# An adaLN attention and gMLP block on one core: gate statistics deferred, another order of the start, part of the transposes by DMA, the last bias by TensorE, the closing branch turned

## The chip, the cores and the metric

One Trainium2 chip, one of its cores. The metric is the device time of one execution in microseconds (us), the median of several runs. A ratio is the mean time of one kernel's fast runs over the mean of the kernel before's fast runs of the same rounds on the same chip, so it isn't quite the ratio of the medians quoted; the brackets behind it are its 95% interval. Times inside a profile are counted from the span's start; the span, first to last instruction, is some 2 us shorter than the device time.

## The reference

```python
mod = (silu(c) @ w_mod)                  # sa, ca, ga, sb, cb, gb: six rows of 512
h = layernorm(x) * (1 + ca) + sa         # x: 2048 x 512 bf16 ("LN1")
q = h @ wq                               # 32 heads of 128; K and V come from a cache, 8 groups
p = softmax(q k^T / sqrt(128)); o = p v  # every query sees all 2048 keys
x = x + ga * (o @ wo)
h = layernorm(x) * (1 + cb) + sb         # "LN2"
z = gelu(h @ w_in)                       # 2048 x 1792: z1 | z2
z2 = layernorm(z2)
g = w_sp @ z2 + b_sp                     # "spatial": mixes the 2048 rows
x = x + gb * ((z1 * g) @ w_out)
```

## The kernel before

A *unit* is 128 rows of queries of one group (four heads). There are 128 units. Each has eight *slots*, and work can be hung onto a slot with `at(unit, slot, fn)`:

```python
    for it in range(NU + 6):                     # NU = 128
        ...
        for i in range(NSLOT):                   # 8 slots
            for fn in later.pop((it, i), []): fn()
            if it < NU: qk(it, i)                # 2 score matmuls, 1 exponential (ScalarE)
            if 1 <= it <= NU: pv(it - 1, i)      # 8 value matmuls of the unit before
            for fn in fill.pop((it, i), []): fn()        # projection matmuls of later q
            if i >= 4 and wf: wf[i - 4]()                # output projection
            if it >= NU: zrun(3)                 # z2 and z1 matmuls fill up the last units
```

What the change touches. The order at the start:

```python
    def ln1_at(it, ch):                          # LN1 of 512 rows, "chunk" ch
        st = {}
        at(it, 1, lambda: st.update(r=ln1_stats(ch * CT, CT)))           # DVE
        at(it, 5, lambda: st.update(x=ln1_norm(ch * CT, CT, st["r"])))   # DVE
        at(it, 7, lambda: ln1_turn(ch * CT, CT, st["x"]))  # PE transposes, PSUM to hT on DVE
    at(0, 0, lambda: ln1_turn(1, CT - 1, xns0))  # rows 128 to 511
    for i in range(NSLOT):
        fill[0, i] = rest0[2 * i : 2 * i + 2]    # their projections
    ln1_at(0, 1); ln1_at(2, 2); ln1_at(5, 3)     # shortened
    at(3, 0, mod_rest)                           # rest of the modulation rows
```

The statistics of z2, straight behind each tile, and the normalisation behind each fourth:

```python
            nc.scalar.activation(out=z2[:, j, :]..., func=ACT.Gelu_apprx_tanh)
            stz = stat.tile([P, NFHC, nc.vector.BN_STATS_DIM], FP32, name="stz")
            for h in range(NFHC):
                nc.vector.bn_stats(out=stz[:, h, :], in_=z2[:, j, h * FC : (h + 1) * FC])
            nc.vector.bn_aggr(out=mvz[:, j, :], in_=stz[:])
    ...
        if j % CT == CT - 1:
            zq[-1] = [zq[-1], lambda ch=j // CT: z2_norm(ch)]
```

The spatial bias, added on VectorE for each tile, and the branch at the end, which runs a slower general path only if a safety flag was set (it isn't for these inputs):

```python
        nc.vector.tensor_tensor(out=gb[:, :n], in0=g_ps[:, :n], in1=bsp_bc[:, cols], op=ALU.add)
        nc.vector.tensor_tensor(out=yT[:, f, c0 : c0 + n], in0=gb[:, :n], in1=z1T[:, f, cols], op=ALU.mult)
    ...
    redo = nc.values_load(flag[0:1, 0:1], min_val=0, max_val=P)
    with tc.If(redo != 0):
        general_path(...)
```

Of the kernel before, what the change touches and what calls it, by code (L numbers as in the profile page):

```python
# [15 lines left out]
P = 128  # L16
# [559 lines left out]
def kernel(  # L576
# [45 lines left out]
    v_dram = A_v_cache[0].rearrange("g (t p) d -> p g t d", p=P)  # L622
    k_rows = A_k_cache[0].rearrange("g (p t) d -> p g t d", p=P)
    v_rows = A_v_cache[0].rearrange("g (p t) d -> p g t d", p=P)
    wmod_dram = w_mod.rearrange("(dt p) n -> p dt n", p=P)
# [72 lines left out]
    k_nat = early.tile([P, SK], BF16, name="kT")  # L698
    nc.sync.dma_start(out=k_nat[:].rearrange("p (t d) -> p t d", d=DH), in_=k_rows[:, 0])
    nc.sync.dma_start(out=x_sb[:, 1:CT, :], in_=x_dram[:, 1:CT, :])  # L700

# [7 lines left out]

    def load_v(g, rows, engine):  # L710
        v1 = late.tile([P, NKT, DV], BF16, name="v1")
        nc.gpsimd.memset(v1[:, :, DH:DV], 1.0)  # L712
        engine.dma_start(out=v1[:, :, 0:DH], in_=rows[:, g])
        groups[g]["v1"] = v1
# [13 lines left out]
    load_wq(0, nc.sync)  # L728
    groups[0] = {}
    load_v(0, v_rows, nc.sync)  # L730
    nc.sync.dma_start(out=x_sb[:, CT : 2 * CT, :], in_=x_dram[:, CT : 2 * CT, :])
    nc.sync.dma_start(out=wmod_b, in_=wmod_dram[:, :, 2 * D : NMOD])
    nc.sync.dma_start(out=x_sb[:, 2 * CT : NT, :], in_=x_dram[:, 2 * CT : NT, :])
    load_wo(0, nc.sync)
    nc.sync.dma_start(out=win_sb[:], in_=win_dram)


    c_f = res.tile([P, NDT], FP32, name="c_f")
    nc.vector.tensor_copy(out=c_f[:], in_=c_bf[:])
# [8 lines left out]
    nc.vector.tensor_copy(out=sc_bf[:], in_=sc[:])  # L748
    nc.vector.memset(ones_bf[:], 1.0)

    def mod_columns(first, wmod, i0):

        mc_ps = bank("o_ps")
        for i in range(2):
            for dt in range(NDT):
                col = i * NDT + dt
                w0 = (first + i - i0) * D + dt * P
                for kt in range(NDT):
                    nc.tensor.matmul(
                        mc_ps[:, col : col + 1],  # L760
                        lhsT=wmod[:, kt, w0 : w0 + P],
                        rhs=sc_bf[:, kt : kt + 1],
                        start=(kt == 0),
                        stop=(kt == NDT - 1),
                    )
        c0 = first * NDT
        nc.vector.tensor_copy(out=modc[:, c0 : c0 + NDT], in_=mc_ps[:, 0:NDT])
        nc.vector.tensor_scalar_add(
            out=modc[:, c0 + NDT : c0 + 2 * NDT], in0=mc_ps[:, NDT : 2 * NDT], scalar1=1.0
        )  # L770
# [14 lines left out]

    def ln1_turn(j0, n, xns):
        ch, c0 = j0 // CT, (j0 % CT) * P
        if ch not in hTs:
            hTs[ch] = res.tile([P, NDT, 512], BF16, name="hT", bufs=NCH)
        hT = hTs[ch]  # L790
        for half in range(2):
            t_ps = bank("misc")[:].bitcast(BF16).rearrange("p (k q) -> p k q", k=2)
            for k in range(2):
                dt = half * 2 + k
                for jj in range(n):
                    nc.tensor.transpose(  # L796
                        t_ps[:, k, jj * P : (jj + 1) * P],
                        xns[jj][:, dt * P : (dt + 1) * P],
                        ident[:],
                    )  # L800
            for k in range(2):
                dt = half * 2 + k
                nc.vector.tensor_scalar(  # L803
                    out=hT[:, dt, c0 : c0 + n * P],
                    in0=t_ps[:, k, 0 : n * P],
                    scalar1=modc[:, NDT + dt : NDT + dt + 1],
                    scalar2=modc[:, dt : dt + 1],
                    op0=ALU.mult,
                    op1=ALU.add,
                )  # L810

    xns0 = ln1_norm(0, 1, ln1_stats(0, 1))
    mod_columns(0, wmod_a, 0)
    ln1_turn(0, 1, xns0)


    kT0 = early.tile([P, SK], BF16, name="kT")
    groups[0]["kT"] = kT0
    k_ps = bank2()[:].bitcast(BF16)
    for kt in range(NKT):  # L820
        nc.tensor.transpose(
            k_ps[:, kt * P : (kt + 1) * P], k_nat[:, kt * P : (kt + 1) * P], ident[:]
        )
    for hf in range(2):
        nc.scalar.copy(
            out=kT0[:, hf * SK // 2 : (hf + 1) * SK // 2],
            in_=k_ps[:, hf * SK // 2 : (hf + 1) * SK // 2],
        )
    rstd0 = ln1_stats(1, CT - 1)

# [28 lines left out]
    for fn in qproj(0, list(range(REP)), 0, P):  # L859
        fn()  # L860
    xns0 = ln1_norm(1, CT - 1, rstd0)

# [126 lines left out]

    def mod_rest():  # L990
        mod_columns(3, wmod_b, 2)
        lhs = []
        for kt in range(NDT):
# [4 lines left out]
            lhs.append(lhs_bc)  # L998
        for row_out, i in ((ga_rows, 2), (gb_rows, 5)):
            mr_ps = bank("misc")  # L1000
            for kt in range(NDT):
                nc.tensor.matmul(
                    mr_ps[:],
                    lhsT=lhs[kt][:],
                    rhs=wmod_b[:, kt, (i - 2) * D : (i - 1) * D],
                    start=(kt == 0),
                    stop=(kt == NDT - 1),
                )
            nc.vector.tensor_copy(out=row_out[:], in_=mr_ps[:])

# [7 lines left out]

    def ln1_at(it, ch):
        st = {}  # L1020
        at(it, 1, lambda: st.update(r=ln1_stats(ch * CT, CT)))
        at(it, 5, lambda: st.update(x=ln1_norm(ch * CT, CT, st["r"])))
        at(it, 7, lambda: ln1_turn(ch * CT, CT, st["x"]))

    fill = {}
    rest0 = qproj(0, list(range(REP)), P, 512 - P)
    at(0, 0, lambda: ln1_turn(1, CT - 1, xns0))
    for i in range(NSLOT):
        fill[0, i] = rest0[2 * i : 2 * i + 2]
    ln1_at(0, 1)  # L1030
    ln1_at(2, 2)
    ln1_at(5, 3)
    at(3, 0, mod_rest)

    def set_fill(b):

        fs = qproj(b, list(range(REP)), 0, 512)
        for k, fn in enumerate(fs):
            it, slot = ((b - 1) * CT + k // NDT, k % NDT) if b > 1 else (1 + k // 8, k % 8)
            fill.setdefault((it, slot), []).append(fn)  # L1040
# [7 lines left out]
    for g in range(1, HKV):  # L1048
        it = (g - 1) * NT + 4
        at(it, 3, lambda g=g: load_k(g))  # L1050
        at(it + 1, 3, lambda g=g: load_v(g, v_dram, nc.gpsimd))
        at(it + 2, 3, lambda g=g: load_wo(g, nc.gpsimd))
# [5 lines left out]
    def z2_tile(j):  # L1058
        ps = {}

        def mm(hf, dt):
# [16 lines left out]
            )  # L1078
            stz = stat.tile([P, NFHC, nc.vector.BN_STATS_DIM], FP32, name="stz")
            for h in range(NFHC):  # L1080
                nc.vector.bn_stats(out=stz[:, h, :], in_=z2[:, j, h * FC : (h + 1) * FC])  # L1081
            nc.vector.bn_aggr(out=mvz[:, j, :], in_=stz[:])

        return [lambda hf=hf, dt=dt: mm(hf, dt) for hf in range(NFHC) for dt in range(NDT)]

    def z2_norm(ch):
# [30 lines left out]
    for j in range(3 * CT):  # L1117
        zq += z2_tile(j)
        if j % CT == CT - 1:
            zq[-1] = [zq[-1], lambda ch=j // CT: z2_norm(ch)]  # L1120
    for f in range(NFT):
        zq += z1_tile(f, 0)
    zq = [z if isinstance(z, list) else [z] for z in zq]

    def zrun(n):
        for _ in range(min(n, len(zq))):
            for fn in zq.pop(0):
                fn()

# [38 lines left out]
    for j in range(3 * CT, NT):  # L1168
        for fn in z2_tile(j):
            fn()  # L1170
    z2_norm(3)
    for f in range(NFT):
# [27 lines left out]

    def spatial(t, yT, f, c0, n):

        g_ps = bank("misc")
        for st in range(NT):
            nc.tensor.matmul(  # L1205
# [3 lines left out]
                start=(st == 0),  # L1209
                stop=(st == NT - 1),  # L1210
            )
        cols = slice(t * 512 + c0, t * 512 + c0 + n)
        gb = mlp.tile([P, 512], BF16, name="gb", bufs=2)
        nc.vector.tensor_tensor(out=gb[:, :n], in0=g_ps[:, :n], in1=bsp_bc[:, cols], op=ALU.add)  # L1214
        nc.vector.tensor_tensor(
            out=yT[:, f, c0 : c0 + n], in0=gb[:, :n], in1=z1T[:, f, cols], op=ALU.mult
        )
# [10 lines left out]
    def finish_tile(t, jj, src, parts=1):  # L1228
# [4 lines left out]
        for k in range(parts):  # L1233
            s = slice(k * w, (k + 1) * w)
            nc.vector.tensor_tensor(out=tmp[:, s], in0=src[:, s], in1=gb_rows[:, s], op=ALU.mult)
            nc.vector.tensor_tensor(out=yout[:, s], in0=tmp[:, s], in1=x_sb[:, j, s], op=ALU.add)
            (nc.sync if k == 0 else nc.scalar).dma_start(out=out_dram[:, j, s], in_=yout[:, s])

# [34 lines left out]
    for f in range(NFT):  # L1273
        spatial(last, yT, f, n_a, P)
        if f == 0:
# [10 lines left out]
    redo = nc.values_load(flag[0:1, 0:1], min_val=0, max_val=P)  # L1286
    with tc.If(redo != 0):
        general_path(
# [33 lines left out]
```

## Time and profile before

| kernel before | us |
|---|---|
| median time (3 runs, 1347.53 to 1349.29) | 1348.0 |
| span of the profiled run | 1345.2 |
| first score of unit 1 starts | 27.66 |
| first score of unit 4 starts | 58.76 |
| first z2 matmul starts | 1150.16 |
| first spatial matmul starts | 1213.63 |
| last VectorE operation ends | 1340.59 |

The rows mark where a part of the program ends. The difference of two kernels from one mark to the next tells where time was won or lost. Where the work of one line on one engine is shown (L1287 is the line of the final branch, SP the sync engine), the columns are line, engine, operation, count, then duration in ns (shortest/median/longest), first and last start in us.

```profile
L1287 SPq EVENT_SEMAPHORE  x8: 17/17/17, 1342.8 to 1343.3; - x8
...
L1287 SPq COMPARE_BRANCH  x1: 53/53/53, 1340.2 to 1340.2; - x1
```

SP branches once at 1340.2, and its next instruction, a semaphore wait, starts at 1342.8. In these 2.6 us the last output DMAs land, so they cost nothing of their own.

### The profile page before, as it was taken

How to read it: one execution, taken by the hardware profiler on the slowest of the kernel's cores; microseconds unless marked ns; L12 is line 12 of the kernel's file. 1: busy time of each engine (PE TensorE's matmuls, PEld its weight loads, DVE VectorE, ACT ScalarE, POOL GpSimd, SP SyncE). 2: the span in 40 equal slices, each digit the busy share in tenths (PEclk: the TensorE clock that was granted, in tenths of full speed). 3: DMA queues.
4: the chain of work that ended last, by engine and by line, in shares of the span. 5: the costliest groups of instructions: out<-in, count | busy, mean ns of one | idle time of the engine just before them, and what ended most of it. 6: DMA issues, size and time to landing. Idle time of an engine off the chain costs nothing.

```text
span 1345.2 us, 27642 instructions
## 1 busy us (share of the span) xinstructions
PE 1303.1 (97%) x12137; PEld 860.4 (64%) x12345; DVE 476.3 (35%) x1171; ACT 1079.2 (80%) x1059; POOL 46.4 (3%) x88
## 2 busy tenths in 40 slices
PE   6999999999999999999999999999999999979997
PEld 4666666666666666666666666666666666534444
DVE  5442222222222222222222222222222666873344
ACT  4789999999999999999999999999999999540000
POOL 1010000000000000000000000000000000110000
PEclk9999999999999999999999999999999999989999
DMA  8120021102211120012010410121111111143200
GB/s 274 29 64 17 13 63 37 21 17 35 62 20 21 32 68 17 17 37 68 17 20 13 84 21 17 21 64 32 21 20 17 29 29 33 25 110 83 67 20 26
DMA packets 141184, 56.53 MB, mean 42 GB/s; under 512 B 131105, under 2 KB 136353, under 8 KB 141057
## 3 DMA queue, kind: packets, MB, share of 16 engines
q1 hardware_dynamic: 137504, 42.17, 15.0%
q0 software_dynamic: 3408, 12.45, 3.5%
q8 instruction: 98, 1.61, 0.5%
q14 instruction: 30, 0.24, 0.1%
q10 hardware_dynamic: 144, 0.07, 0.0%
HBM read 21.63 MB, written 2.10 MB: 18 GB/s over the span
## 4 chain that ended last, share of the span: by engine, by line
PE 92%; DVE 3%; SPq 2%; issue 1%; DMA 1%; POOL 0%; ACT 0%; ACTq 0%; POOLq 0%; DVEq 0%
PE s_ps L879 35%; PE o_ps L901 34%; PE misc L843 7%; PE misc L933 6%; PE misc L1205 6%; PE s_ps L1100 2%; SPq L1012 1%; PE o_ps L1220 1%; PE s_ps L1064 1%; DMA wq_g<-in_A_wq_dram 1%; DVE stz L1081 1%; DVE hT L803 0%; PE s_ps L1220 0%; PE misc L796 0%; DVE bnst L690 0%
## 5 line engine op out<-in xcount | busy, mean ns | idle before, releaser
L886 ACT ACTIVATE pT<-s_ps 128x1024 bf16<-128x1024 f32 x1024 | 1045.6, 1024 | 92.2 <-PE s_ps L879 16.5
L901 PEld LDWEIGHTS <-pT 128*128 128x128 bf16 x8192 | 548.5, 98 | 241.2
L901 PE MATMUL o_ps<-v,pT 128*128 128x129 bf16 x8192 | 631.4, 220 | 0.0
L879 PE MATMUL s_ps<-qT,kT 128*128 128x512 bf16 x2048 | 609.9, 379 | 10.8 <-DVE qT L852 0.8
L912 DVE RECIPROCAL rall<-o_ps 128x2 f32<-128x2 f32 x256 | 43.6, 170 | 750.9 <-PE o_ps L901 750.7
L879 PEld LDWEIGHTS <-kT 128*128 128x128 bf16 x2048 | 199.8, 98 | 120.1 <-issue 1.3
L843 PE MATMUL misc<-hT,wq_g 128*128 128x512 bf16 (+2 forms) x462 | 169.1, 376 | 0.8 <-DMA wq_g<-in_A_wq_dram 0.8
L933 PE MATMUL misc<-wo_g,oT 128*128 128x512 bf16 x386 | 146.3, 379 | 0.0
L913 DVE TENSOR_TENSOR onorm<-o_ps,rall 128x256 bf16<-128x256 f32 x256 | 108.7, 425 | 8.8
L1205 PE MATMUL misc<-wsp,z 128*128 128x512 bf16 (+2 forms) x555 | 100.5, 336 | 1.8 <-DVE gb L1214 1.3
L852 DVE CAST qT<-misc 128x512 bf16<-128x512 f32 (+1 forms) x129 | 87.2, 676 | 1.0 <-PE misc L843 1.0
L1205 PEld LDWEIGHTS <-z 128*128 128x128 bf16 x560 | 50.7, 98 | 50.3 <-issue 1.8
L946 DVE TENSOR_TENSOR xacc<-misc,xacc 128x512 f32<-128x512 f32 x112 | 76.2, 680 | 0.0
L843 PEld LDWEIGHTS <-wq_g 128*128 128x128 bf16 x528 | 51.8, 99 | 3.6 <-DMA wq_g<-in_A_wq_dram 1.0
L933 PEld LDWEIGHTS <-oT 128*128 128x128 bf16 x512 | 50.1, 98 | 0.7
L1214 DVE TENSOR_TENSOR gb<-misc,bsp_bc 128x512 bf16<-128x512 f32 (+2 forms) x35 | 20.4, 584 | 60.9 <-PE misc L1205 60.9
L1100 PE MATMUL s_ps<-hT,win_sb 128*128 128x512 bf16 x109 | 26.5, 401 | 7.3 <-ACT z1T L1108 7.1
L1108 ACT ACTIVATE z1T<-s_ps 128x1024 bf16<-128x1024 f32 x14 | 14.2, 1024 | 19.5 <-PE s_ps L1100 10.9
L1064 PE MATMUL s_ps<-win_sb,hT 128*128 128x448 bf16 x128 | 27.0, 352 | 0.1
L1074 ACT ACTIVATE z<-s_ps 128x896 bf16<-128x896 f32 x16 | 14.7, 917 | 14.9 <-PE s_ps L1064 14.9
L712 POOL MEMSET v<- 128x128 bf16 x8 | 1.6, 205 | 705.9 <-issue 606.9
L1100 PEld LDWEIGHTS <-win_sb 128*128 128x128 bf16 x112 | 11.5, 102 | 21.9 <-issue 10.1
(68 smaller groups left out, 288.6 us busy)
## 6 DMA issues: line engine op xcount, KB each, us to landing
v<-in_A_v_cache_dram POOLq DMA_DIRECT2D x7, 512.0 KB, 6.6
wo_g<-in_A_wo_dram POOLq DMA_DIRECT2D x7, 512.0 KB, 4.8
wq_g<-in_A_wq_dram POOLq DMA_DIRECT2D x7, 512.0 KB, 6.0
wsp<-in_w_mod_dram SPq DMA_DIRECT2D x1, 2048.0 KB, 9.2
oT<-onorm SPq DMA_TRANSPOSE x128, 2.4
out_dram<-yout SPq DMA_DIRECT2D x15, 128.0 KB, 1.7
win_sb<-in_B_w_in_dram SPq DMA_DIRECT2D x1, 1792.0 KB, 13.6
wmod_a<-in_w_mod_dram SPq DMA_DIRECT2D x1, 1024.0 KB, 5.4
```

The costliest lines, as they stand in the source:

```text
L843: nc.tensor.matmul(ps[0][:, o0 : o0 + n], lhsT=wqs[g][:, dt, hh * DH : (hh + 1) * DH], rhs=hTs[ch][:, dt, c0 : c0 + n], start=(dt == 0), s ...
L852: nc.vector.tensor_copy(out=qTs[b][:, hs[0] : hs[-1] + 1, c0 : c0 + n], in_=ps[0][:, 0 : len(hs) * n].rearrange("p (h q) -> p h q", q=n),)
L879: nc.tensor.matmul(s_ps[:, h * 512 : (h + 1) * 512].rearrange("p (r q) -> p r q", r=REP), lhsT=groups[g]["kT"][:, kt * P : (kt + 1) * P], ...
L886: nc.scalar.activation(out=pTs[u][:, 2 * i : 2 * i + 2, :], in_=s_ps[:].rearrange("p (k q) -> p k q", k=2), func=ACT.Exp, scale=inv_sqrt_dh,)
L901: nc.tensor.matmul(o_ps[:, hh % 2, 0 : DH + 1], lhsT=pTs[u][:, kt, hh * P : (hh + 1) * P], rhs=groups[g]["v1"][:, kt, 0 : DH + 1], start=( ...
L912: nc.vector.reciprocal(out=rall[:, c0 : c0 + 2], in_=o_ps[:, :, DH])
L913: nc.vector.tensor_tensor(out=onorms[u][:, hh - 1 : hh + 1, :], in0=o_ps[:, :, 0:DH], in1=rall[:, c0 : c0 + 2].unsqueeze(2).to_broadcast([ ...
L933: nc.tensor.matmul(X_ps[:], lhsT=oTs[u][:, hh, :], rhs=groups[g]["wo"][:, hh, :], start=(hh == 0), stop=(hh == REP - 1),)
L946: nc.vector.tensor_tensor(out=xaccs[j][:], in0=X_ps[:], in1=xaccs[j][:], op=ALU.add)
L1064: nc.tensor.matmul(ps[0][:, hf * 512 : hf * 512 + FC], lhsT=h2Ts[j // CT][:, dt, (j % CT) * P : (j % CT + 1) * P], rhs=win_sb[:, dt, FH + ...
L1100: nc.tensor.matmul(ps[0][:, k * 512 : (k + 1) * 512], lhsT=win_sb[:, dt, f * P : (f + 1) * P], rhs=h2Ts[2 * ch2 + k][:, dt, :], start=(dt ...
L1205: nc.tensor.matmul(g_ps[:, :n], lhsT=z2[:, st, f * P : (f + 1) * P], rhs=wsp[t][:, st, c0 : c0 + n], start=(st == 0), stop=(st == NT - 1),)
```

## The change

Its intent: start the first scores sooner (one tile of rows first, then three; half of K turned by DMA, so that wq arrives earlier; PE warmed by idle matmuls). Turn the later LN1 chunks by DMA rather than on PE. Issue big loads later. Take z2's statistics off VectorE's queue where attention ends. Add the bias of the very last columns by a one-row matmul. Its core, cut:

```diff
-    nc.sync.dma_start(out=k_nat[:]..., in_=k_rows[:, 0])
-    nc.sync.dma_start(out=x_sb[:, 1:CT, :], in_=x_dram[:, 1:CT, :])
+    nc.sync.dma_start(out=k_nat[:, 0:HK]..., in_=k_rows)
     ... load_wq(0, nc.sync) ...
+    nc.sync.dma_start(out=x_sb[:, 1:CT, :], in_=x_dram[:, 1:CT, :])
+    nc.sync.dma_start_transpose(out=kT0[:, HK:SK], in_=A_k_cache[0, 0, HK:SK])
     ...
+    warm(18)
     xns0 = ln1_norm(0, 1, ln1_stats(0, 1))
     mod_columns(0, wmod_a, 0)
-    ln1_turn(0, 1, xns0)
+    ln1_turn(0, 1, xns0, on_act=(1, 3))
     ... 8 instead of 16 K transposes on PE ...
+    warm(3)
     ...
-    at(0, 0, lambda: ln1_turn(1, CT - 1, xns0))
+    at(0, 3, lambda: ln1_turn(1, CT - 1, rest0["xn"]))
+    for k, fn in enumerate(rest_q):
+        fill.setdefault((0, 5 + min(k // 5, 2)), []).append(fn)
+    # ln1_at(chunk, statistics, normalisation, turn or modulation):
+    # chunks 2 and 3: DMA transposes one slot behind norm, modulation at the last place
+    ln1_at(1, (0, 7), (1, 3), (1, 6))
+    ln1_at(2, (1, 7), (2, 2), (3, 5))
+    ln1_at(3, (4, 1), (4, 5), (5, 5))
+    at(2, 5, lambda: nc.gpsimd.dma_start(out=wmod_b, in_=wmod_dram[:, :, 2 * D : NMOD]))
+    at(5, 5, lambda: nc.gpsimd.dma_start(out=win_sb[:], in_=win_dram))
+    # modulation matmuls now in units 9, 10, 11
     ...
-            it, slot = ... if b > 1 else (1 + k // 8, k % 8)
+            it, slot = ... if b > 1 else (2 + k // 8, k % 8)
     ...
+    at(NU + 1, 7, lambda: z2_stats(0))
+    ... z2_stats(1) to (11), spread up to (NU + 5, 4) ...
+    for ch in range(3):
+        at(NU + 5, 5 + ch, lambda ch=ch: z2_norm(ch))
     ...
+        if bias_by_pe:                       # only the last 128 columns
+            nc.tensor.matmul(g_ps[:, :n], lhsT=ones_bf[0:1, :], rhs=bsp_bc[0:1, cols], start=False, stop=True)
     ...
-    with tc.If(redo != 0):
+    with tc.If(redo != 0, preferred_fallthrough_block=False):
```

## The prediction

> **What bounds the kernel now.** I read the busy table by stretch first, then the chain that ended last, the waits, and the timeline where these point. A *unit* below is one pass of the attention loop (128 rows, four heads, one key group): eight slots, each with two score matmuls, eight value matmuls and usually one projection matmul.
>
> ```profile
> core 0: us, PE busy (x) PEld busy (x) DVE busy (x) ACT busy (x) POOL busy (x), PEclk, DMA share, GB/s
> ...
> 5.00:10.00 5.00, 2.73 (x50) 2.60 (x51) 2.60 (x10) 0.00 (x0) 0.81 (x2) 1.00 1.05 386
> 200.00:1100.00 900.00, 891.97 (x8844) 610.75 (x8996) 263.33 (x662) 837.10 (x819) 19.15 (x32) 1.00 0.16 32
> 1180.00:1240.00 60.00, 54.89 (x246) 24.99 (x251) 30.41 (x69) 17.89 (x18) 5.01 (x8) 0.94 0.44 99
> ```
>
> From 200 to 1100 us TensorE is busy 892 of 900: the loop is bound by PE and the change takes little from it. What can be won is PE idleness at the start, at a few interruptions of the first units, where attention ends, and in the tail.
>
> The chain, in order of time, shows the start and one slot of the loop:
>
> ```profile
> 3.28 7.95 DMA wq_g<-in_A_wq_dram
> 11.28 1.90 PE misc L843 x16
> ...
> 13.89 0.33 DVE xn L679
> ...
> 15.56 1.64 DVE hT L803 x4
> ...
> 21.88 1.38 DVE xn L679 x4
> ...
> 27.66 0.60 PE s_ps L879 x2
> ...
> 36.63 0.43 PE s_ps L879 x2
> 37.07 0.45 PE o_ps L901 x8
> 37.52 0.22 PE misc L843
> ```
>
> The first projection waits for wq until 11.23. Unit 1, the first with value matmuls, begins at 27.66, after LN1 turns of rows 128 to 1023. From there a slot costs 0.43+0.45+0.22 = 1.10 us of PE, a unit 8.8; without the projection matmul 0.88, less than the 1.03 us of ScalarE's exponential (1024 ns in its group), which then sets the pace.
>
> The timeline after unit 2 (start, duration), then the waits:
>
> ```profile
> 44.18 0.61 PE L796 MATMUL misc<-ident,xn 128*128 128x128 bf16 x8
> ...
> 45.88 0.62 PE L796 MATMUL misc<-ident,xn 128*128 128x128 bf16 x8 [1.09 <-DVE hT L803]
> ...
> 47.44 0.94 PE L759 MATMUL o_ps<-sc_bf,wsp 128*128 128x1 bf16 x32
> ...
> 50.76 0.59 PE L879 MATMUL s_ps<-qT,kT 128*128 128x512 bf16 x2
> ```
>
> ```profile
> ACT z1T L1108 <- DVE x_sb L952: 8.6, 1, 8.6
> ...
> PE s_ps L1100 <- ACT z1T L1108: 7.1, 1, 7.1
> ```
>
> The LN1 turn of rows 1024 to 1535 keeps score matmuls off PE from 44.18 to 46.34, the modulation rows from 47.44 to 50.76. At 1177.7 PE stops for 7.1 us: the first z1 activation reuses attention's memory, free only when x_sb of the last tile is written (1183.53). That VectorE chain was late because the z2 statistics (1.15+0.21 us a tile) and normalisations stood ahead of it.
>
> **What the Trainium skill says.** "TensorE: Matmul & The Clock Gate", Part 1: PE starts at half clock, warms after about 4 us of activity, and drops back after an idle window of about 3.4 us. The trace agrees: the 16 matmuls at 11.28 took 1.90 us, some 107 ns each, while transposes at 44.18 come 56 ns apart; after the 7.1 us stop, 15 matmuls took 4.83 us, 322 ns each, against 216 before. "VectorE: DVE Perf Modes", Why PSUM operands drop a tier: a PSUM operand slows an operation. Here the 128x128 bias addition from PSUM took 289 ns, the product from SBUF 225. "Runtime: NRT & Kernel Launch", Instruction fetch mechanics: a taken branch out of the fetched window costs a fetch. Here ScalarE's final compare-and-branch starts at 1341.6 and its next instruction at 1344.3.
>
> **The change part by part.**
>
> *Start, to unit 1.* wq now follows 256 KB of K instead of 512 KB and no longer the 384 KB of x. The old order moved 1.18 MB by 7.2 us and 2.62 MB by 11.2, some 360 GB/s; 1.97 MB is then down at about 9.5. Eighteen idle matmuls warm PE before wmod arrives at 7.27. Then 32 column matmuls (0.9), four transposes, eight K transposes (0.45), three warming matmuls, and 16 projections at 56 ns from 9.85; the 0.69 us cast ends at 11.6. Scores start at 11.65, against 15.96. But rows 128 to 511 come after: statistics 3 x 0.80 to 14.0, GpSimd's rstd (0.23+0.89) to 15.3, three normalisations of 0.35 to 16.4, turns to 17.05; slot 3 stands behind them in PE's order. Slots 3 to 7 with 16 projections of 384 columns (0.1625 each) end at 22.7.
>
> The new order of VectorE's instructions then has a trap: the statistics of rows 512 to 1023 (slot 7, 4 x 0.80 = 3.2 us) stand after the second and before the third of the four casts that unit 1 reads. Second cast to 21.65, statistics to 24.85, two casts of 0.55 to 25.95. Unit 1 starts at 26.0: gain 1.65, where the PE work alone would give 4.2.
>
> *Units 1 to 11.* New unit 1 has no projection and is paced by exponentials, 8 x 1.03, its PE turn of 0.9 mostly hidden: 8.35. Unit 2: 8.8. Unit 3 has eight projection and four output matmuls, 9.65. The last projection now sits in slot 7 of unit 3, and unit 4's first score needs its cast behind an onorm pair (0.62+0.69 plus handover): 1.15 lost. Unit 4 starts at 26.0+8.35+8.8+9.65+1.15 = 53.95, before at 58.76: gain 4.8, including the 1.65. The turn of the last 512 rows (2.16, 75.27 to 77.43) moves to DMA transposes and short SBUF operations: +2.15. The modulation matmuls come back in units 9 to 11: 0.94+1.90 less drains, -2.65. Sum to unit 12: **4.3**.
>
> *Big loads postponed* (win, second half of wmod). No PE wait named them: 0. The eight transposes on the sync queue (1.2 us of issue each) land about ten us before use: 0.
>
> *Deferred statistics.* PE times before this point stay, so on the old clock the last output projection ends at 1169.0. VectorE's new order: chain of tile 126 at 1165.6 to 1168.6, two deferred statistics of 1.3, normalisation and modulation 1.4, tile 127's chain 1172.6 to 1174.8. The first z1 activation is due at 1175.8: no stop. Saved: 7.3 between matmuls, plus 15 x (322-216) = 1.6 of cold clock, and 0.3 of smaller gaps: **9.2**. The deferred work must still fit: five statistics and three normalisations end at about 1195.2, four more statistics at 1200.4, the last normalisation at 1203.7. The spatial matmuls start at 1204.3, instead of 1213.63, and need the last z2 tile 3.2 us later.
>
> *Last bias by PE.* Seven 128-column matmuls with one row (56 ns, +0.4 of PE) replace seven additions; the product now reads PSUM and costs some 0.29 instead of 0.23. VectorE saves about 0.2 per tile, but it is held by three finish operations of 1.4 each. Following it through: last product at 1337.7 instead of 1338.2. **0.6**.
>
> *Branch direction*, in the diff though not in its title. The no-repair case falls through but must then jump over the repair code: the far fetch stays, and on the sync engine now comes after the output DMAs' completion instead of beside it: **-0.4**.
>
> Sum 4.3+9.2+0.6-0.4 = 13.7; less 0.3 for the clock (below): 13.4. 1348.0-13.4 = **1334.6 us**.
>
> **Rivals.** *A, the stop at 1177 only shrinks.* VectorE carries 7 us of work in a unit of 5.4 us of PE just there; my margin for the x_sb chain is 1 us. For: before, the same queue was late by 8. Against: nine of the twelve statistics move behind that chain. If it slips 3 us, PE stops some 2 us, without going cold: 1337; if wholly, 1344. *B, the start gives its full 4.2 and more*, because statistics slip in earlier than I have them, or nothing stands behind the exponentials: 1331. Against: VectorE runs in order, and the casts stand after the statistics. *C, the start gives nothing*: the idle gap ahead of unit 1 (22.7 to 26.0, 3.3 us) reaches the window after which PE goes cold, 1.5 us more, or x of the later chunks comes late behind the transposing K load, whose speed next to plain loads no row shows: 1337 to 1339. I weigh the cold clock at one in five: 0.3. *D, hidden by PE*: only the idle at 1177 counts and the loop takes all else back: 1339.
>
> **Range and chances.** The 9.2 is firm to about 1.5 if A fails; the 4.3 may be 1 to 7; tail and branch are within 1 each. 8 in 10: 1329.5 to 1340.5. Two per cent is 27 us, and all PE idleness outside the loop before (my estimate from the stretches: about 17 to unit 1, 12 at the change of phase, 9 in the tail) is 38, much of it out of the change's reach: faster 0.03, same 0.96, slower 0.01.
>
> **What would show it.** First scores near 11.7; a VectorE wait of some 3 us on PE's side ahead of unit 1 at 26; no 2.2 us holes in units 2 and 5, one of about 1 us ahead of unit 4; no stop before the z1 matmuls, PE clock full there; spatial matmuls starting some 13.5 us earlier in the trace (near 1200); the tail from first 128-column spatial matmul to last output operation 0.5 shorter. I am wrong if the z1 matmuls still wait for x_sb, if unit 1 starts before 24 or after 28, or if spatial matmuls wait for normalised z2.

## The result, and the profile after

The changed kernel is correct and takes 1339.45 us (four runs, 1338.44 to 1340.88), the kernel before in the same rounds 1347.98: ratio 0.9936 [0.9919, 0.9953], 0.6% less. That is the same by the measure of 2%, inside the predicted range and 4.9 us above the predicted time. The two profiled spans differ by 7.6 us, and the marks part them:

| mark | before | after | gain up to here | predicted |
|---|---|---|---|---|
| first score of unit 1 starts | 27.66 | 26.98 | 0.7 | 1.65 |
| first score of unit 4 starts | 58.76 | 56.31 | 2.45 | 4.8 |
| unit 6 ends (last reciprocal) | 87.32 | 83.42 | 3.9 | 6.95 |
| unit 12 ends | 140.16 | 138.79 | 1.4 | 4.3 |
| first z2 matmul | 1150.16 | 1148.78 | 1.4 | 4.3 |
| first spatial matmul | 1213.63 | 1202.93 | 10.7 | 13.5 |
| last VectorE operation ends | 1340.59 | 1329.36 | 11.2 | 14.1 |
| span ends | 1345.2 | 1337.6 | 7.6 | 13.7 |

Two pieces fell short, each by some 3 us: the start (1.4 instead of 4.3) and the very end, where 3.6 us are lost after the last VectorE operation.

**The start.** The chain of the changed kernel, in order of time (start, duration):

```profile
19.91 1.39 PE misc L885 x5
...
22.26 0.56 DVE qT L894
22.82 0.61 DVE bnst L691
...
26.02 0.92 DVE qT L894 x2
26.98 0.60 PE s_ps L922 x2
...
28.16 0.85 PE s_ps L922 x2
29.01 0.87 PE o_ps L944 x8
```

The order foreseen is there: the second cast (22.26), four statistics (22.82 to 26.0), the last two casts (26.02), then unit 1. But five projections took 1.39 us, and in unit 1 a pair of scores takes 0.85 and a group of value matmuls 0.87 instead of 0.43 and 0.45. PE runs at half pace. The table by stretch shows a lower clock; its columns are the stretch, its length, busy time of five engines, granted PE clock, DMA share and GB/s:

```profile
core 0: us, PE busy (x) PEld busy (x) DVE busy (x) ACT busy (x) POOL busy (x), PEclk, DMA share, GB/s
...
20.00:35.00 15.00, 11.97 (x97) 7.85 (x96) 7.45 (x19) 8.95 (x9) 1.27 (x2) 0.85 0.00 1
...
1180.00:1240.00 60.00, 59.68 (x277) 27.59 (x282) 34.03 (x74) 14.75 (x15) 4.50 (x6) 1.00 0.43 91
```

The granted clock from 20 to 35 is 0.85. In finer stretches it is 0.50 from 18 to 20, 1.00 from 22 to 27 and 0.50 from 29 to 31: two drops, one before and one after the wait for the casts. From 1180 to 1240 it is 1.00 and PE is busy 59.68 of 60 us, where before it was busy 54.89 at 0.94.

**DMA transposes.** A wait (total, times, longest), and the DMA table (median us from issue to landing):

```profile
DVE hT L815 <- DMA hT<-xn: 9.1, 2, 6.6
```

```profile
oT<-onorm SPq DMA_TRANSPOSE x128, 2.4
...
hT<-xn SPq DMA_TRANSPOSE x8, 8.7
```

The eight new transposes land after 8.7 us, while the kernel's old transposes of the same size, 128x512, take 2.4. VectorE's modulation stands in its queue waiting for them for 2.5 and 6.6 us. PE feels the second ahead of unit 6, in the PE timeline (unit 4's start to unit 6's end gained 1.45 us by the marks, 0.7 less than predicted):

```profile
79.32 0.61 PE L944 MATMUL o_ps<-v,pT 128*128 128x129 bf16 x8 [0.38 <-DVE onorm L956]
```

**Where attention ends.** The chain has no stop any more. The z1 matmuls (L1158) follow the last z2 group, and the spatial ones (L1273) follow those:

```profile
1167.76 5.11 PE s_ps L1119 x27
1172.87 0.22 PE s_ps L1158
...
1173.14 10.74 PE s_ps L1158 x49
...
1203.10 1.51 PE misc L1273 x7
```

49 matmuls in 10.74 us are 219 ns each; before, 15 of them took 322 each behind a stop of 7.1 us.

**The end.** What the branch's line (now L1361) does on SP, and the first instructions behind the repair code (L1391):

```profile
L1361 SPq EVENT_SEMAPHORE  x8: 17/17/17, 1329.1 to 1331.9; - x8
...
L1361 SPq COMPARE_BRANCH  x2: 38/48/57, 1329.0 to 1332.2; - x2
```

```profile
L1391 SPq EVENT_SEMAPHORE  x14: 17/28/28, 1336.0 to 1337.6; - x14
```

SP falls through its first branch (1329.0), waits till 1331.9 for the output to land, and only then, at 1332.2, takes the second branch over the repair code. Its next instruction starts at 1336.0, 3.8 us later. Before, the taken branch came first, at 1340.2, and its 2.6 us lay beside the landing of the output. From the last VectorE operation to the span's end: 4.6 us before, 8.2 after.

### The profile page after: what moved, and what is told of

The parts are those of the page before. It is cut to its first block, busy times and chain, and to the rows that moved or that the text cites. A ratio compares the mean times of both kernels' runs of the same rounds, so it can differ in the third digit from the quotient of the medians.

```text
span 1337.6 us, 27647 instructions
## 1 busy us (share of the span) xinstructions
PE 1305.1 (98%) x12126; PEld 859.4 (64%) x12333; DVE 473.1 (35%) x1163; ACT 1079.3 (81%) x1060; POOL 48.6 (4%) x90
## 3 DMA queue, kind: packets, MB, share of 16 engines
q1 hardware_dynamic: 141888, 39.29, 15.7%
## 4 chain that ended last, share of the span: by engine, by line
PE 94%; SPq 2%; DVE 1%; issue 1%; DMA 1%; POOL 0%; ACT 0%; DVEq 0%
PE s_ps L922 35%; PE o_ps L944 35%; PE misc L885 7%; PE misc L976 6%; PE misc L1273 6%; PE s_ps L1119 2%; PE s_ps L1158 2%; SPq L1056 1%; PE o_ps L1294 1%; PE s_ps L1294 0%; DMA wmod_a<-in_w_mod_dram 0%; DMA hT<-xn 0%; DVE bnst L691 0%; DVE qT L894 0%; DMA out_dram<-yout 0%
## 5 line engine op out<-in xcount | busy, mean ns | idle before, releaser
L1273 PE MATMUL misc<-wsp,z 128*128 128x512 bf16 (+2 forms) x555 | 100.5, 336 | 1.7 <-DVE gb L1288 1.1
L1273 PEld LDWEIGHTS <-z 128*128 128x128 bf16 x560 | 50.7, 98 | 49.5 <-issue 1.0
L1288 DVE TENSOR_TENSOR gb<-misc,bsp_bc 128x512 bf16<-128x512 f32 (+1 forms) x28 | 18.4, 658 | 53.1 <-PE misc L1273 53.1
L1158 PE MATMUL s_ps<-hT,win_sb 128*128 128x512 bf16 x109 | 24.3, 379 | 0.2
L691 DVE BATCH_NORM_STATS2 bnst<-x_sb 128x6 f32<-128x512 bf16 x32 | 21.8, 682 | 0.5
```

The source lines that it names most:

```text
L1158: nc.tensor.matmul(ps[0][:, k * 512 : (k + 1) * 512], lhsT=win_sb[:, dt, f * P : (f + 1) * P], rhs=h2Ts[2 * ch2 + k][:, dt, :], start=(dt ...
L1273: nc.tensor.matmul(g_ps[:, :n], lhsT=z2[:, st, f * P : (f + 1) * P], rhs=wsp[t][:, st, c0 : c0 + n], start=(st == 0), stop=(st == NT - 1 a ...
```

## The experiments

Twelve kernels, in four groups that each ran on one chip beside the kernel before. Each is the changed kernel with the edit shown, unless said otherwise. The changed kernel itself ran in other rounds. Its time is compared by medians, and the kernel before's median lay between 1347.2 and 1348.0 in the five sets of rounds, so such a difference carries up to 0.8 us of that. "Mark" is the start of the last reciprocal of a unit, as in the table above.

### The branch (e1, e2)

```diff
-    with tc.If(redo != 0, preferred_fallthrough_block=False):
+    with tc.If(redo != 0):
```

> The changed kernel with the closing branch in its old direction (the repair code is the fall-through again). In the changed kernel's trace the sync engine waits for the output DMAs to 1332.2, then jumps, and its next instruction comes at 1336.0; in the kernel before it jumped at 1340.2, was over by 1342.8 and waited for the DMAs only then. Theory: the far jump is paid either way, but in the changed kernel it stands after the completion of the outputs, so undoing it gives 3 to 4 us: about 1336.0, and from the last VectorE operation to the end of the span 4.6 us instead of 8.2. Rival: the longer end is a coincidence of this run (a slow fetch): then the time stays at 1339.4, and the end stays near 8 us.

Measured: 1336.59 us (1335.63 to 1336.87), ratio 0.9915 [0.9898, 0.9932], 2.9 below the changed kernel. The branch's line on SP:

```profile
L1361 SPq EVENT_SEMAPHORE  x8: 17/17/17, 1332.4 to 1332.9; - x8
...
L1361 SPq COMPARE_BRANCH  x1: 53/53/53, 1329.8 to 1329.8; - x1
```

One branch again, and the 2.6 us again beside the output DMA. The last VectorE operation ends at 1330.15 and the span at 1334.8, so the end is 4.65 long, as before.

The opposite edit, in the kernel before:

```diff
-    with tc.If(redo != 0):
+    with tc.If(redo != 0, preferred_fallthrough_block=False):
```

> The kernel before with the branch direction of the change and nothing else. Theory: 3 to 4 us slower, about 1351.5, with 8.2 us from the last VectorE operation to the end. Rival: the end of the changed kernel is long because of something else in it (for example the order of its DMA semaphores): then this stays at 1348.0.

Measured: 1350.05 us, ratio 1.0014 [0.9998, 1.0031], 2.1 more than the kernel before in the same rounds (1347.96). SP branches at 1340.8 and at 1344.1, and 7.15 us lie between the last VectorE operation and the end. The interval just reaches 1, but all four runs lie above all seven of the kernel before, and the end is 2.5 us longer in the profile. The theory's 3 to 4 us and 8.2 us were too high. The direction costs 2.1 us in the kernel before and 2.9 in the changed one (3.6 in its profiles); its sign and place are shown both ways. From the second branch to SP's next instruction it is 2.6 us here and between 2.6 and 3.8 in the ten profiles with this direction; the changed kernel's is the longest.

### Unit 1: statistics behind the casts (e3)

```diff
-    ln1_at(1, (0, 7), (1, 3), (1, 6))
+    ln1_at(1, (1, 0), (1, 4), (1, 7))
```

> The changed kernel with the statistics of rows 512 to 1023 moved from slot 7 of unit 0 to slot 0 of unit 1, behind the four casts that unit 1 reads (its normalisation to slot 4, its turn to slot 7). Theory: the 3.2 us of statistics are what unit 1 waits for, and the 3.0 us of PE idleness they cause also drop PE's clock for some 3.6 us. Unit 1's first score then at about 24.2 instead of 26.98, its slots at 1.03 us instead of up to 1.7, no dent in the granted clock of that stretch; gain 2.8+1.3 = about 4, 1335.4. Rival 1: only the wait goes, the clock drops for the earlier idle gap in unit 0: gain 2.7. Rival 2: the casts are late for another reason (PE, banks): gain under 1.

Measured: 1336.07 us (1335.29 to 1336.55), ratio 0.9912 [0.9895, 0.9928], 3.4 below the changed kernel. Unit 1's first score comes at 24.53 instead of 26.98, and the granted clock from 20 to 35 is 1.00. At the mark of unit 1's middle the gain is 4.1, at unit 12 still 3.3. So the statistics stood in unit 1's way. That the pause they make lets the clock drop fits too: of the nine profiles with a pause of 3.0 us there, eight show half clock behind it (all but e5's), and of the three without it (e3, e10, e12) none. The earlier drop, which rival 1 names, is there in e3 too (0.57 from 16 to 20). Part was given back in units 4 and 6, where VectorE waited for the DMA transposes for 10.1 us in sum.

### The deferred statistics (e4)

```diff
             nc.scalar.activation(... func=ACT.Gelu_apprx_tanh)
+            z2_stats(j)                 # and z2_norm(ch) behind each fourth tile
-    at(NU + 1, 7, lambda: z2_stats(0))  # and all others of that list
```

> The changed kernel with the z2 statistics and normalisations back where they were, right behind each z2 tile. Theory: the stop of 7.1 us before the third z1 tile and the cold clock after it return, 9.2 us slower than the changed kernel: about 1348.6, that is no better than the kernel before. Rival: part of the 9.3 us that the change won there comes from the other parts (less VectorE work near it): then under 7 us slower.

Measured: 1349.16 us, ratio 1.0011 [0.9994, 1.0027], 9.7 above the changed kernel. The stop is back, among the waits:

```profile
ACT z1T L1167 <- DVE x_sb L995: 8.6, 1, 8.6
...
PE s_ps L1159 <- ACT z1T L1167: 7.1, 1, 7.1
```

Both are the figures of the kernel before, to the tenth. The deferral alone carries more than the whole net gain.

### Chunk 1's projections spread (e5)

The last cast of chunk 1 stood on unit 4's path, because the last projection came in slot 7 of unit 3.

```diff
-    ... else (2 + k // 8, k % 8)
+    ... else (2 + (k * 3 // 4) // 8, (k * 3 // 4) % 8)
```

> The changed kernel with the 16 projection matmuls of the second 512 rows spread over twelve slots (the last in slot 3 of unit 3 instead of slot 7). Theory: in the changed kernel unit 4's first score waits for the last cast, behind value matmuls, reciprocal and onorm (chain at 55.03 to 56.31, 1.3 us beyond the last matmul of unit 3); with four slots between, this wait goes: no DVE qT entry in the chain at unit 4 and 1.0 to 1.3 us off, 1338.3. Rival: the chain only moves to the modulation of hT, which also comes late there (2.5 us of VectorE waiting for the DMA transposes): then less than 0.4.

Measured: 1338.46 us (1336.95 to 1340.85), ratio 0.9939 [0.9926, 0.9953]: nothing in time. In its profile the cast is off the path and unit 4 gains 1.3 by the marks, but 1.1 of it is lost at unit 6, where the chain now runs through a DMA transpose of 11.5 us. What comes sooner waits longer for the same transposes.

This profile shows something more. Its program is the changed kernel's up to unit 1, yet its clock was 1.00 from 16 to 35, and unit 1's first score came at 26.05, within 0.05 of the predicted 26.0 (e6 and e7 below, at full pace up to there too, have 25.93 and 25.87). The changed kernel's later 26.98 is therefore the slower clock from 16 on, and nothing in the order.

### The loads moved apart (e6)

```diff
-    at(2, 5, lambda: nc.gpsimd.dma_start(out=wmod_b, ...))
-    at(5, 5, lambda: nc.gpsimd.dma_start(out=win_sb[:], in_=win_dram))
+    at(6, 5, lambda: nc.gpsimd.dma_start(out=wmod_b, ...))
+    at(12, 5, lambda: nc.gpsimd.dma_start(out=win_sb[:], in_=win_dram))
```

> The changed kernel with the two big gpsimd loads moved away from the DMA transposes of LN1: the second half of wmod to unit 6, win to unit 12. In the changed kernel these eight transposes took 8.7 us from issue to landing (median), where the 128 of oT take 2.4, and VectorE waited 2.5 and 6.6 us for them; the second wait delays the start of unit 6 by 0.7 us on PE. Theory: the big loads of 2.0 and 1.8 MB share the DMA engines; apart from them the transposes land in about 3 us, both waits vanish, and 0.7 us is won (1338.7). Rival: four transposes in a row on one queue are slow by themselves, or the loads of v and K near them do it: landing stays above 6 us and the time the same.

Measured: 1350.11 us (1348.84 to 1354.1), ratio 1.0027 [1.0014, 1.0041], 10.7 *above* the changed kernel. The waits:

```profile
DVE hT L815 <- DMA hT<-xn: 14.2, 1, 14.2
...
PE o_ps L944 <- DVE onorm L956: 8.0, 1, 8.0
```

The edit did one half of what it was made for. These are the landing times (shortest/median/longest) of the first four transposes, issued from 41.72, and of the second four, issued from 62.39:

```profile
DMA to landing us min/median/max: 2.4/2.4/2.4
```

```profile
DMA to landing us min/median/max: 7.4/15.7/18.6
```

In the changed kernel they are 6.1/8.3/8.9 and 5.1/10.8/13.2. The first four no longer have the second half of wmod (2 MB) beside them and land in 2.4 us each, so four in a row on one queue aren't slow by themselves. That part of the rival is out.

The second four have more beside them than before, because GpSimd's queue isn't held by units: once its last waiting operation (the rstd of chunk 3) is done, it issues every load queued behind. Five loads (5.25 MB) were issued between 61.69 and 65.37 (v, wo, wmod_b, wq, win), where the changed kernel had four (3.25 MB) there. The expected time was missed with the wrong sign. The run still shows the mechanism, with the dose turned down and up: less load beside the transposes, earlier landing; more load, later landing, and PE held.

### The bias, and the warming (e7, e8)

```diff
-        spatial(last, yT, f, n_a, P, bias_by_pe=True)
+        spatial(last, yT, f, n_a, P)
```

> The changed kernel with the last bias added by VectorE again. Theory: the part is worth 0.6 us, since the three finish operations of 1.4 us hold VectorE anyway: 1340.0, and the stretch from the first 128-column spatial matmul to the end of the last output operation 12.65 us as in the kernel before, against 12.2. Rival 1: VectorE's seven additions of 0.29 us all stand on the path: 2 us slower. Rival 2: nothing.

Measured: 1339.73 us (1337.33 to 1340.67), ratio 0.9940 [0.9926, 0.9953]. In the trace the last VectorE operation ends at 1329.97 instead of 1329.36, but 0.36 us of that is there already where the 128-column matmuls begin (1317.35 and 1316.99), before the edit acts. The stretch from there to the end is 12.62 us, in the changed kernel 12.37 and in the kernel before 12.65. So the part is worth 0.25 to 0.3, and the times can't tell that from nothing. It has a cost that was overlooked: with the one-row matmul the tiles start 1.37 us apart on PE instead of 1.11, so it costs 0.26 each and not 0.056. The part gains all the same, as PE's waits for VectorE in this stretch (0.21 and 1.10 in e7's timeline) go.

```diff
-    warm(18)
-    warm(3)
```

> The changed kernel without the idle matmuls that warm PE (18 at the start, 3 before the first projection). Theory: PE then runs K transposes, projection, first scores, turns and the 384-column projections of unit 0 at half clock (107 ns instead of 56 for 128 columns), so the first scores come about 1.3 us later and unit 1 some 2 to 3 us later: 1341.5 to 1342.5. Rival: PE is not what unit 0 waits for (statistics, exponentials), and it cools before unit 1 in any case: under 1 us.

Measured: 1342.43 us (1340.21 to 1344.01), ratio 0.9964 [0.9949, 0.9979], 3.0 above the changed kernel by the medians and 3.8 by the ratios. Unit 1's middle comes 1.8 later and unit 12's end 2.5 later. The first scores come 0.7 later, not 1.3. The idle matmuls are worth their place; the prediction has them inside its start, without a figure of their own. A trap in reading: in this profile the granted clock is given as 1.00 from 12 to 25, yet the twelve transposes take 1.89 us instead of 1.38. The column doesn't show the slow pace with which PE begins.

### Who waits for the late transposes (e9)

```diff
-    ln1_at(3, (4, 1), (4, 5), (5, 5))
+    ln1_at(3, (4, 1), (4, 5), (7, 5))
```

> The changed kernel with one thing moved: the modulation of rows 1536 to 2047, which waits on VectorE for the late DMA transposes, goes from slot 5 of unit 5 to slot 5 of unit 7 (its first reader is in unit 8). Theory (the transposes landing late block VectorE's queue, and that alone cost PE 0.7 us at the start of unit 6): VectorE's 6.6 us wait for hT is gone or under 1 us, the reciprocal at the end of unit 6 comes 0.5 to 0.9 us earlier than 83.42 by the marks, time 1338.8, ratio to the kernel before 0.9930. Rival (PE's 0.7 us come from something else, such as the o_ps turn of unit 5): mark and time as in the changed kernel, 1339.4.

Measured: 1340.3 us (1339.15 to 1341.72), ratio 0.9938 [0.9924, 0.9951], no gain. VectorE's longer wait is gone, as expected, and yet unit 6 ends at 83.75 (changed kernel: 83.42). The SP timeline shows the DMA issues, and the PE timeline the new wait:

```profile
63.31 10.92 SPq L855 DMA_TRANSPOSE hT<-xn  x4
74.33 3.40 SPq L964 DMA_TRANSPOSE oT<-onorm  x2
```

```profile
80.23 0.39 PE L976 MATMUL misc<-wo_g,oT 128*128 128x512 bf16 x1 [0.50 <-DMA oT<-onorm]
```

The four hT transposes hold SP's queue for 10.9 us. The transposes of oT, which the output projection needs, stand behind them, and now PE waits for those. My theory that VectorE's block alone was the cost is wrong. The cost is the slow transposes; taking one waiter away brings up the next.

### The DMA turns undone (e11)

```diff
-        if ch == 1:
+        if ch > 0:            # PE turns chunks 2 and 3 too
     ...
-    ln1_at(2, (1, 7), (2, 2), (3, 5))
-    ln1_at(3, (4, 1), (4, 5), (5, 5))
+    ln1_at(2, (1, 7), (2, 2), (2, 7))
+    ln1_at(3, (4, 1), (4, 5), (4, 7))
```

> The changed kernel with rows 1024 to 2047 turned by PE again (64 transposes of 128x128, PSUM to hT on VectorE), at slot 7 of units 2 and 4; the eight DMA transposes go. Theory (each turn keeps score matmuls off PE for some 2.2 us as in the kernel before, and the late DMA transposes cost the changed kernel only 0.7 to 1): the mark at the end of unit 6 comes 3 us later than 83.42, time 1342.5, ratio 0.9960. Rival (in the changed kernel these units wait for exponentials and casts anyway, so the turns fit in): under 1 us, 1339.5 to 1340.5.

Measured: 1343.45 us (1342.37 to 1343.89), ratio 0.9964 [0.995, 0.9977], 4.0 above the changed kernel. Unit 6 ends 4.75 later; 1.1 of that was there by the middle of unit 1, where this run's clock was lower (0.61 from 25 to 30, against 0.78), so about 3.6 belongs to the turns. Turning by DMA is worth its waits.

### All of it together (e10), and a bridged pause (e12)

The edits of e1, e3, e5 and e9, and the two big loads issued on the sync queue, where they stand behind the oT transposes of their unit and so can't start early:

```diff
-    at(2, 5, lambda: nc.gpsimd.dma_start(out=wmod_b, ...))
-    at(5, 5, lambda: nc.gpsimd.dma_start(out=win_sb[:], in_=win_dram))
+    at(6, 5, lambda: nc.sync.dma_start(out=wmod_b, ...))
+    at(12, 5, lambda: nc.sync.dma_start(out=win_sb[:], in_=win_dram))
```

> The changed kernel with all that the runs so far showed to cost: the default branch direction (-2.9 alone), statistics of rows 512 to 1023 behind the fourth cast (-3.4 alone), projections of chunk 1 spread so that the last cast isn't on unit 4's path (-1.2 by unit 4), the last modulation in unit 7, and the two big loads (second half of wmod, win) issued on the sync queue behind the oT transposes of units 6 and 12, where they can't start beside the hT transposes. Theory (the costs are separate and add up): 1331, within 1329.5 to 1332.5, ratio 0.9875; no cold clock before unit 1; hT transposes land within some 6 us in units 2 and 4. Rival (what is won early is given back at the hT transposes as in the spread run): 1333 to 1334, ratio 0.9895.

Measured: 1331.15 us (1330.43 to 1332.12), ratio 0.9872 [0.9856, 0.9887], as expected. The two gains measured alone (2.9 and 3.4) make 1333.1; by difference, the other 2 us come from the parts that showed no gain alone. The first four hT transposes land in 2.4 us each. The second four still have v, wo and wq (1.5 MB) beside them and take 8.7 (5.9 to 10.8), more than the expected 6, but VectorE has no wait for them, as their modulation comes later. From unit 3's middle (47.77) to the end of unit 6 (78.59) PE takes 30.8 us for three and a half units, 8.8 each: nothing is lost there. In the changed kernel the same stretch took 33.6.

The start of this run still shows PE at half pace, so one more line:

```diff
+    at(0, 3, lambda: warm(6))     # ahead of the turn of rows 128 to 511
     at(0, 3, lambda: ln1_turn(1, CT - 1, rest0["xn"]))
```

> The combined version with one line more: six idle matmuls of 512 columns between the third pair of scores of unit 0 and the LN1 turn of rows 128 to 511, where PE idled 1.86 us and after which it ran at half pace until about 22 (twelve transposes 1.89 us instead of 1.38, a pair of scores 1.01 instead of 0.59). They wait for the exponential of slot 1 (about 14.5), so PE's pause shrinks to 0.4 and 0.3. Theory (these pauses let the clock drop, and the slow matmuls stand on the path to unit 1): granted clock 1.00 from 16 to 25, unit 1's first score at 24.5 instead of 25.66, time 1329.8, ratio 0.9863. Rival (the drop is not made by this pause, as the granted clock falls in some profiles and not in others of the same start): no change within run scatter, 1331, ratio 0.9872, or later by up to 1 us where the idle matmuls delay the transposes.

Measured: 1329.56 us (1329.33 to 1330.01), ratio 0.9869 [0.9852, 0.9885]. PE's timeline, first without and then with the line:

```profile
15.98 1.89 PE L833 MATMUL misc<-ident,xn 128*128 128x128 bf16 x12 [1.86 <-DVE xn L680]
...
25.66 0.61 PE L922 MATMUL s_ps<-qT,kT 128*128 128x512 bf16 x2 [0.65 <-DVE qT L894]
```

```profile
14.50 1.46 PE L766 MATMUL s_ps<-onorm 128*128 128x512 bf16 x6 [0.32 <-ACT pT L929]
16.03 1.38 PE L833 MATMUL misc<-ident,xn 128*128 128x128 bf16 x12
...
23.66 0.60 PE L922 MATMUL s_ps<-qT,kT 128*128 128x512 bf16 x2 [0.65 <-DVE qT L894]
```

The pause of 1.86 us is filled, the same twelve transposes take 1.38 instead of 1.89 us, and unit 1 starts 2.0 us earlier, which is kept to unit 12 (131.95 against 133.96). All four runs had a mean granted clock of 0.998 or 0.999, those of e10 0.996 or 0.997. Of the ten other profiles with this pause and a warmed start, seven show the drop behind it and three don't (e5, e6, e7), so the one profile alone wouldn't prove the cause; the clocks of all four runs speak for it. What it is worth in time isn't settled: the medians differ by 1.6, but the kernel before was also 0.8 faster on that chip, and the ratios differ by 0.4 us only, less than their intervals.

## Why the prediction was right, and where its steps were not

The class and the range held. The reason is that the largest term held; the start and the branch were mis-sized, both towards too much gain. The branch missed its own margin of 1 us by more than 2, and the range, made wide for other risks, took that in: this much is luck.

**Deferred statistics: right.** Predicted 9.2 at the change of phase; the marks give 10.7 - 1.4 = 9.3, and undoing it costs 9.7. The stop was found on the chain, its cause in VectorE's queue, and rival A (a stop that only shrinks) didn't come: PE is busy 59.68 of the 60 us.

**Start to unit 1: the order right, the clock missed.** First scores were predicted at 11.65 and came at 11.77. The statistics between the second and the third cast, the wait of 3 us and a start of unit 1 at 26.0 were foreseen. With a clock of 1.00, as in e5's profile, it was 26.05. The clock cost about 1.0 us ahead of unit 1 in the changed kernel's profile; the further 1.35 by unit 4 is what is left of the gap to the prediction, and I put it down to the clock as well. The second drop is rival C as written: half clock behind a pause of 3.0 us ahead of unit 1. I weighed it at one in five and put 0.3 us into the sum; it came in eight of the nine profiles that have the pause. The first drop, from about 18 on, nobody foresaw: it came after pauses of 0.7 to 1.9 us.

**Units 2 to 6: one term missing.** The 1.15 ahead of unit 4 (the cast behind an onorm pair) was there, and e5 took it away. "The eight transposes land about ten us before use: 0" was the wrong step: I took the landing time of oT's transposes, which mostly run alone, for those of hT, which run beside loads. Measured 8.7 us instead of 2.4 (2.4 in e6 without a load), up to 5.6 us for one issue on SP instead of 1.2, and 0.7 us of PE at unit 6. "Big loads postponed: 0" failed for the same reason. I took the unit in which a load is written for the time at which GpSimd issues it. So 4.3 became 1.4: less 1.0 and 1.35, put down to the clock, and 0.7 of late transposes. The modulation's return in units 9 to 11 was right (-2.65 predicted, -2.5 by the marks).

**Last bias: right sign, half the size.** 0.6 predicted, 0.25 to 0.3 measured in its stretch, below what the times resolve. The added matmul costs PE 0.26 us a tile instead of 0.056. The product from PSUM took 0.29, as predicted; its 289 ns against 225 compares fp32 with bf16 as well as PSUM with SBUF.

**Branch: right sign, wrong size.** -0.4 predicted, -3.6 in the profile, -2.9 by undoing it. The mechanism was named word for word (a far fetch that comes after the output's completion instead of beside it). But I charged only a fraction of a fetch, where the view of the branch in the kernel before already had its size: 2.6 us on SP. What stood beside the output's landing then stands behind it whole, and on SP it took 3.8. The instruction queues move data in both pauses (before 1339.9 to 1342.9: four packets; after 1332.2 to 1336.1: five), which fits a fetch; whose fetch it was, the profile doesn't say.

In the two profiles: 1.4 + 9.3 + 0.5 - 3.6 = 7.6, the difference of the spans; 0.5 is the gain from the first spatial matmul to the last VectorE operation, of which 0.28 lie in the bias's stretch. Why PE cooled in some profiles of the same start and not in others stays open. One reading in the prediction needs a word: 16 matmuls in 1.90 us are 119 ns each; its 107 is the distance of their starts, with the last one's duration (some 0.3 us) taken off.

## What to carry to other kernels

The time lay in one queue's order: statistics ahead of a critical chain on VectorE cost 9 us of PE. The busy table shows that PE idles there (54.89 busy of 60 us), but not why. A load written late in the program isn't issued late if its engine's queue has nothing to wait for; put it behind something that the loop itself releases. And what overlaps the last output DMA is free only as long as it stays beside it, so a change of a branch's direction is to be read on the engine that waits for that DMA.

## What the Trainium skill lacked or had wrong

- "Runtime: NRT & Kernel Launch", Instruction fetch mechanics, says that a taken branch out of the fetched window forces a DMA fetch, without a size. On the sync engine the runs show 2.6 us from a taken branch to the next instruction when it lay beside the output DMA (kernel before and e1), and 2.6 (e2) to 3.8 us (changed kernel) where it came after it.
- "TensorE: Matmul & The Clock Gate", Part 1, has PE drop to half clock after an idle window of about 3.4 us that runs freely; that frequent short pauses can do it too stands there without a size. Here it dropped without one pause that long: PE was busy 1.46 of 4.00 us from 12 to 16, its longest pause was 1.86 us, and the granted clock from 16 to 20 was 0.69 (changed kernel) and 0.50 (e10). With 2.95 of 4.00 us busy (e12) it was 1.00, and in the profiles of e5, e6 and e7 it stayed at 1.00 with 1.46 to 1.51 busy.
- "DMA: Bandwidth & Descriptors", Rules for kernel authors, says of corrupted data that a transpose next to ordinary DMAs needs nothing, and the results here were correct. No page that I read has what the neighbours cost in time: four 128x512 transposes landed in 2.4 us each with no load beside them (e6), in a median of 8.3 beside 2 MB (changed kernel), 8.7 beside 1.5 MB (e10), 10.8 beside 3.25 MB (changed kernel) and 15.7 beside 5.25 MB (e6), and four of them held the sync queue for 10.9 us (e9).
- No page that I read spells out for loads what separate instruction streams imply: GpSimd issues its queued loads as soon as nothing ahead of them waits, whatever the program around them does. Five loads were issued within 3.7 us in e6, though written into different units.
